# A fused recurrence and MLP kernel on Trainium2: part of the transfers issued by ScalarE, some of them joined, and a new order of all steps

## The chip, the core and the metric

The kernel runs on one core of a Trainium2 chip. The core has a matrix engine (TensorE, "PE", with its weight loads as "PEld"), three engines for elementwise work (VectorE, "DVE"; ScalarE, "ACT"; GpSimd, "POOL") and SyncE ("SP"), which here does nothing but issue transfers. Each engine takes its own instructions in the order in which the program lists them and waits for others through semaphores. Transfers are carried out by 16 DMA engines; an instruction of SP, ACT or POOL issues each of them. The metric is the device time of one execution in microseconds. In the profile L1119 is line 1119 of the kernel.

## What is computed

The inputs are r, k, v, w, a, b with shape (4, 8, 768, 40): batch, heads, time, head size. For each batch and head a 40 x 40 state runs through 768 time steps; the output of all heads, 320 numbers for each of 3072 tokens, goes through an MLP with exact GELU:

```python
for t in range(S):
    y[:, :, t] = np.einsum('bhd,bhde->bhe', rt, state)
    Sa = np.einsum('bhde,bhe->bhd', state, at)
    state_decay = state * wt[:, :, None, :] - np.einsum('bhd,bhe->bhde', Sa, bt)
    state = state_decay + np.einsum('bhd,bhe->bhde', vt, kt)
...
h = x @ w_in                                  # 3072 x 320 by 320 x 2048
g = 0.5 * h * (1.0 + erf(h * inv_sqrt2))
return (g @ w_out).astype(np.float32)         # by 2048 x 320
```

The attention inputs are float32. The MLP's weights arrive as float64 and are taken apart into words and rebuilt as float32 on the core.

## The kernel before

The 768 steps are cut into 12 chunks (c = 0 to 11) of 64. Within a chunk the recurrence is put into matrix form, which needs the inverse of a triangular 64 x 64 matrix for every batch and head. That inverse is made of inverses of 32 x 32 blocks. The work is written as many small *steps*, Python generators that yield wherever another step may be put in between. A token such as `ph3:0` advances step `ph` of chunk 3 by one piece; the number behind the colon names the pair of PSUM banks (0 to 3) that the piece takes. The string ORDER (L30) lists all tokens. The loop at L1231 walks through it, so ORDER sets the order of instructions on every engine. Nothing else schedules.

The steps that matter below, with what they do for chunk c:

- `w`, `a`, `b`, `k`, `v`, `r` (L231 to L277) load inputs; `vp`, `wq`, `bp`, `kp` (L280 to L295) load them again as pairs of time steps, for turned copies that DVE makes in `tv`, `wt`, `tb`, `tk`, `ta`, `tr`. `wi`, `wl`, `wo` load the words of the MLP's weights; `ci` and `co` (to_float, L452) convert them on DVE and ACT.
- `logs`, `sums`, `wt`: logarithms (Ln) of the decays, their running sums, and exponentials (Exp) on ACT. Each change among Ln, Exp and Gelu loads a table on ACT.
- `N`: 32 small products, a masking on DVE (L676), and stores of the 32 x 32 blocks to DRAM (L715). `nb` (L784) loads them back with one block on each partition; `inv` (L788) inverts all of them on POOL in 31 pairs of operations (L799, L801) and stores the result to DRAM (L808, issued by POOL from c = 3 on); `ft` (L822, L826) loads it into Tt. `corner` and `joined` finish the 64 x 64 inverse on PE, DVE and ACT.
- For chunk 0 the inverse is made on PE, DVE and ACT by repeated squaring instead (`sq`, `cornerd`, `joinedd`), since nothing else is there to do yet.
- `A`, `av`, `X`, `sa`, `saT`, `RV`, `M`, `tn`, `yy`, `QY`, `qk`: the products of the recurrence. `state` carries the state to the next chunk.
- `y` (L1041) multiplies the result by the decays on DVE into xt, then shifts parts of it between partitions, so that 320 values fill five groups of 64 partitions: for chunks 1 to 11 with 11 transfers from xt to xt, three at L1071 and eight of 16 KB at L1076. For chunk 0 PE does this.
- `ph` (L1111): the MLP's first product, 64 x 128 tiles in 8 pieces a chunk (L1119), each two followed by GELU on ACT (L1122).
- `po` (L1134): the second product. For chunks 0 and 1 it is plain (L1141); from chunk 2 on seven products of half size and additions on DVE (L1157, L1161 to L1199) take the place of eight. `store` (L1128) writes the output.
- `warm` (L1214): one matrix product whose result nobody reads; `begin`: six of them at the start.

All transfers are issued by SP, except the store of the inverse (POOL from c = 3 on) and six moves of `y11`, which ACT issues. SP takes them in the order of ORDER: one that must wait for its data or for its target to be free holds all that are listed behind it.

Of the kernel before, what the change touches and what calls it, by code (L numbers as in the profile page):

```python
# [10 lines left out]
FP32 = mybir.dt.float32  # L11
# [8 lines left out]
WORDS_BY_ACT = False  # L20
COPIED_BY_ACT = (1, 2)
MOVED_BY_ACT = (11,)
# [11 lines left out]
sq1 sq0 sq1:2 k1 sq0 sq1 warm1:1 N1 sq1 sk0 ci0:0 wi0 sq1:0 N1 ci0 sq1 tr0:1 sq1 ci0 tk0:2 wi0 tk0 sk1 wi0 sq0:3 sq1  # L34
sq0 tr0 A0:2 ci1:1 sq1:0 sq0 ci1 sq1 sq0 nb1 sq1 A0 sq1 wi0 sq0:1 wi0 sq0 RV0:3 sq0 RV0 sq0 wl1 sq1:0 wl1 sq1 inv1 r2
sq0:2 sq1 sq1 sq0 tk1:1 sq0 sq0 sq1:3 tk1 w2 sq1 sq0:0 sq0 cornerd0 placed2 av0:2 ci2:2 placed3 cornerd0:3 ci1 ci2
inv1 nb1 placed1 warm0:1 cornerd0 wl0 ci3:0 wl0 av0 av0:0 r1 ci2 joinedd0:1 av0 joinedd0 tr2:3 placed0 joinedd0 tr2
warm2:2 wi1 a2 ci3 sa0:0 sa0 sa0:1 inv1 sa0 b2 warm5:2 ci4:1 ci9:2 ci4 QY0:3:0 logs2 ci4 k2 qk0 warm7:2 ci9 y0 warm3:1
wi1 state0 wi1 A1:2 wi1 A1 wi1 sums2:1 wi1 inv1 ci9 wo2 sums2:0 sums2 ci3 tv1:3 tv1 tr1:2 sc2 sums2 tn1:0 ci5:1 tn1
ta2:3 ta2 ci5 av1:1 tr1 ci5 sk2 inv1 y0:0 tb2:3 wi1 inv2 ci7:2 tb2 wo6 zeros6 y0:2 ci7 zeros7 y0 y0 tk2:3 av1 ci6:0  # L40
N2:2 ci6 N2 ft1 tk2 co3:1 ph0:0 ft1 ci6 wi1 ph0 corner1:0 N2 ci7 X1:1 corner1:2 corner1 ft1 ph0 X1 ph0:3 wo0 ci8:0
co2:2 ci8 RV1:2 RV1 nb2 warm4:1 ci8 joined1:0 wo9 joined1 wq3 ph0 co0:0 joined1 co0 inv2 ph0 co0 v2 ph0:1 co2 co3
co1:0 sa1:2 co1 sa1 w3 co1 saT1:0 saT1 co3 ph0 co2 wo4 ph0 inv2 ph0:3 co6:0 wt3:1 co6 co7:2 ph0 vp3 co7 ph0 co7
yy1:2:0 logs3 M1:1 M1 tv2:3 wt3 co6 wo8 sums3:1 nb2 sums3 wt3 QY1 zeros5 a3 inv3 tv2 qk1 co4:2 y1 wo15 po0:1 inv2
co5:0 y1 state1 co5 co4 po0 co5 RV2:3 wo10 A2:0 co4 y1 tn2:2 A2 tn2 co9:0 po0 ta3 co9 wt3 inv2 co15:2 bp3 po0 co9 co15
av2:0 co11:1 kp3 co8:0 co11 av2 co11 ph1:2 co8 co8 wo14 inv2 ph1 co10:1 tb3 co10 ph1 wo13 ph1:0 co10 a4 ph1 RV2 ph1
inv4 ft2 co14:0 ph1:2 ta3 co14 wo12 ft2 co14 ft2 N3:3 co15 X2:0 k4 X2 ph1 corner2:1 co13:0 corner2:0 N3 corner2 co13
co12:2 N3 po0 co13 co12 joined2:0 tables0 joined2 k3 joined2 po0 ta4 ph1 co12 sa2:3 nb3 tables0 saT2:0 tk3:1 b3 sa2
sk3 saT2 po0 r3 inv3 yy2:2:3 po0 po0 M2:0 po0 nb3 M2 po0 tv3 ph1:1 inv3 po0 tr3 wq4 ph1 sc3 QY2 w4 qk2 y2 po1:0 state2
bp4 inv3 po1 logs4 b4 A3:2 y2 A3 X3:3 wt4:0 po1 wt4 v3 ph1 wt4 po1 y2 inv3 wt4 po1 po1 ta4 kp4 po1 inv3 vp4 av3:2 tb4  # L50
av3 sums4:1 po1 X3 po1 RV3:2 v4 ws0 sums4 N4:3 N4 inv5 sk4 RV3 ph2:1 N4 sc4 tk4:2 ph2 ft3 ph2 ft3 ph2:3 ws3 nb4 ws1
nb4 ph2 corner3:1 ph2 ft3 ph2:2 inv4 a5 corner3:1 corner3 w5 ph2 ph2 joined3:3 joined3 r4 tn3:1 joined3 tn3 inv4
saT3:3 saT3 sa3:2 sa3 logs5 po1 ph2:1 ta5 bp5 yy3:3:2 M3:0 M3 inv4 tv4 ph2 ph2 tr4 wq5 QY3 qk3 po2:0 po1 sums5:0 sums5
y3 po1 po2:1 state3 y3 po2 inv4 wt5:2 RV4:0 po2:1 po2 wt5 k5 A4:2 po2 A4 tn4:3 y3 tn4 wt5 po2:1 tables1 wt5 po2 po2
inv4 kp5 av4:2 tb5 av4 X4:3 po2 ph3:2 sk5 X4 a6 po2 ta5 ph3 v5 RV4 N5:3 N5 ws2 po2:1 N5 po2 ft4 po2 ph3 ft4 ph3:0 ft4
corner4:0 nb5 tk5:2 ph3 vp5 ph3 corner4:3 ta6 corner4 inv5 nb5 po2 po2:1 po2 joined4:2 joined4 joined4 ph3:0 b5 saT4:3
saT4 sa4:1 r5 inv5 sa4 ph3 ph3 sc5 ph3:2 w6 yy4:3:1 M4:0 M4 tv5 ph3 inv5 ph3 tr5 wq6 QY4 logs6 po3:1 qk4 bp6 state4
po3:0 kp6 y4 po3 po3:2 wt6:0 A5:2 po2 sums6:1 A5 wt6 inv6 k6 inv5 sums6 wt6 y4 po3 wt6 po3 po3:3 po3 po3 tn5:2 y4 tn5
av5:1 tb6 RV5:0 po3 av5 po3 po3:2 ta6 b6 po3 inv5 po3 a7 N6:1 X5:3 N6 X5 N6 sk6 ph4:2 RV5 tk6:1 ph4 ph4 ft5 ta7 ph4:1
ft5 sc6 ft5 A6:3 corner5:0 nb6 r6 inv6 po3 po3:0 po3 corner5:2 A6 corner5 ph4 joined5:0 joined5 ph4 joined5 ph4:2 vp6  # L60
sa5:3 sa5 saT5:0 saT5 inv6 ph4 nb6 ph4 yy5:1:3 w7 M5:0 tr6 tv6 ph4:2 M5 wq7 ph4 inv6 ph4 QY5 v6 logs7 po4:2 qk5 po3 y5
bp7 po4:0 wt7:1 state5 wt7 po4 kp7 po4:0 av6:2 inv7 av6 y5 inv6 wt7 po4 po4 po4:1 wt7 po4 po4 v7 sums7:3 X6:2 y5 po4
ta7 sums7 tb7 po4 po4:0 po4 a8 X6 N7:3 inv6 N7 RV6:1 tk7:2 N7 ph5:2 po4 k7 ph5 ph5 ph5:3 ft6 nb7 ph5 ft6 ph5 nb7
corner6:0 ph5:0 RV6 ft6 inv7 corner6:2 po4 corner6 tn6:3 r7 tn6 po4:1 po4 joined6:2 ta8 joined6 joined6 ph5 inv7 vp7
ph5 sa6:3 sa6 saT6:1 saT6 ph5:2 po4 yy6:0:3 bp8 M6:1 M6 inv7 tr7 ph5 ph5 tv7 QY6 po5:1 wq8 qk6 y6 po5:1 state6 y6 po5
po5:2 inv7 po5 wt8:0 A7:2 y6 RV7:0 A7 wt8 tn7:3 RV7 tn7 wt8 vp8 inv7 po5 po5:1 po5 wt8 po5 X7:2 av7:0 inv8 av7 tb8 sk7
kp8 po5 ta8 b7 inv9 po5 po5:3 po5 a9 po5 N8:0 N8 ft7 ph6:1 N8 ph6 ph6 ft7 ta9 ph6:3 ft7 corner7:1 X7 ph6 tk8:2 nb8 ph6
corner7:0 nb8 corner7 sc7 ph6:1 r8 inv8 joined7:2 joined7 joined7 po5 po5:3 po5 sa7:0 sa7 saT7:2 saT7 bp9 ph6 inv8 po5
ph6 ph6:3 w8 yy7:0:2 M7:1 M7 tv8 ph6 ph6 wq9 inv8 QY7 logs8 po6:0 qk7 tr8 v8 state7 po6:1 y7 v9 po6 wt9:1 tn8:3 y7 tn8
A8:0 inv8 A8 wt9 X8:2 sums8:3 po6:2 po6 sums8 wt9 y7 po6 po6:0 po6 wt9 po6 av8:1 av8 kp9 RV8:3 po6 tb9 b8 inv8 po6  # L70
# [10 lines left out]
corner10 po9:2 vp11 po9:2 joined10:3 joined10 joined10 po9 nb11 sa10:0 inv11 sa10 r11 saT10:1 po9:1 saT10 tn10:3 tn10
po9 po9 po9:0 yy10:1:3 v11 M10:2 M10 tv11 po9 inv11 po9 po9 logs11 QY10 qk10 y10 po9 po9:2 y10 state10 po9 po9 X11:0
y10 sums11:1 sums11 A11:3 A11 inv11 po9 po9:2 po9 tn11:1 tr11 tn11 av11:3 po9 av11 RV11:2 X11 b11 inv11 RV11 ph10:1
k11 ph10 ph10 sc11 ph10:3 sk11 ft11 ph10 ft11 ph10 ft11 ph10:0 corner11:0 ph10 ph10 corner11:2 corner11 ph10:1
joined11:3 joined11 joined11 ph10 ph10 saT11:0 saT11 po10:2 po10:2 yy11:3:1 M11:0 M11 po10 po10:1 po10 QY11 po10 qk11
y11 po10:0 y11 po10 po10 y11 po10 y11 po10 po10:2 y11 y11 y11 po10 y11 po10 po10 po10:1 po10 po10 ph11:3 ph11 ph11
ph11:0 ph11 ph11 ph11:2 ph11 ph11 ph11:1 ph11 ph11 po11:0 po11:3 po11 po11:2 po11 po11 po11:0 po11 po11 po11 po11
po11:2 po11 po11 po11 po11:1 po11 po11
"""


@with_exitstack
def kernel(
    ctx: ExitStack,
    tc: tile.TileContext,
    r: bass.AP,
# [100 lines left out]

    raws = {}  # L200
# [1067 lines left out]
```

## Time and profile before

| | |
|---|---|
| runs of the kernel before | 668.63, 669.81 and 672.28 us |
| their median | 669.81 us |
| profiled execution, first to last instruction (span) | 661.8 us |
| median above that span | 8.0 us |
| granted TensorE clock over the span | 0.999 |
| transfers issued by SP, ACT and POOL | 774, 6 and 18 |
| bytes moved | 79.41 MB, mean 120 GB/s |

The profile of one execution tells only its span; the 8.0 us are what lies around it, by the runs. The page gives each engine's busy time; issuing a transfer is not counted as busy, but the timeline has it as rows of SPq and ACTq. Waits are listed by who waited for whom, with the total, the number and the longest. A row of the timeline has the start, the time to its last end, engine, line, operation, output and inputs, shape, and how many instructions it joins. One float32 product stands there as two instructions. Its end is modelled and reaches into the next product, so the distance from one row's start to the next row's is the better price.

### The profile page before, as it was taken

The page shows a single profiled execution, that of the slowest core. Times are in us where ns is not written, and L with a number is a line of the kernel's source. Part 1 is how long each engine was busy: PE and PEld are TensorE (multiplying, and loading weights), DVE is VectorE, ACT ScalarE, POOL GpSimd, SP SyncE. Part 2 cuts the span into 40 slices and gives each one's busy share as a digit, 9 for nine tenths or more (in the row PEclk, how much of TensorE's full clock was granted, in tenths as well). Part 3 has the DMA queues.
Part 4 walks back from the last instruction along what each step waited for, and adds up shares of the span by engine and source line. Part 5 has one row for each costly group of instructions (what it writes and reads, how often), then busy time and mean ns, then how long its engine had stood idle before and what let it go on. Part 6 is the DMA issues. An engine that isn't in the chain of part 4 may idle for free.

```text
span 661.8 us, 30753 instructions
## 1 busy us (share of the span) xinstructions
PE 646.7 (98%) x13768; PEld 567.3 (86%) x13768; DVE 416.0 (63%) x536; ACT 239.3 (36%) x305; POOL 367.7 (56%) x799
## 2 busy tenths in 40 slices
PE   8889999999999999999999999999999999999997
PEld 4777788777778988998998998998988999998987
DVE  1778989976483874983863963863765674632313
ACT  4355646432424622522522422515253242232020
POOL 6158536706857837846838836847823874840000
PEclk9999999999999999999999999999999999999999
DMA  9989675696676476764775485675685465450100
GB/s 136 164 192 176 158 167 132 153 159 146 116 132 134 105 137 134 140 116 112 145 141 107 94 153 124 119 147 110 115 146 111 103 121 102 86 101 3 42 1 21
DMA packets 300708, 79.41 MB, mean 120 GB/s; under 512 B 288584, under 2 KB 293328, under 8 KB 300576
## 3 DMA queue, kind: packets, MB, share of 16 engines
q1 hardware_dynamic: 299512, 74.92, 58.3%
q0 software_dynamic: 864, 2.36, 1.8%
q8 instruction: 108, 1.77, 1.1%
q14 instruction: 24, 0.20, 0.1%
q10 hardware_dynamic: 200, 0.16, 0.1%
HBM read 64.09 MB, written 9.70 MB: 112 GB/s over the span
## 4 chain that ended last, share of the span: by engine, by line
PE 82%; DVE 8%; SPq 5%; issue 2%; DMA 1%; ACT 0%; DVEq 0%; ACTq 0%
PE duo L1119 29%; PE duo L149 25%; PE duo L1157 22%; PE duo L1141 4%; PE duo L557 2%; SPq L213 2%; SPq L227 1%; DVE conv L466 1%; SPq L1076 1%; DVE conv L472 1%; DMA spare<-in_a_dram 1%; DVE conv L458 1%; DVE conv L457 1%; DVE aT L588 1%; DMA rows<-in_b_dram 0%
## 5 line engine op out<-in xcount | busy, mean ns | idle before, releaser
L1119 PE MATMUL duo<-xt,w_in_sb 64*128 64x256 f32 x1920 | 218.8, 381 | 1.4 <-issue 1.4
L1119 PEld LDWEIGHTS duo<-xt,w_in_sb 64*128 64x128 f32 x1920 | 182.5, 187 | 23.9 <-issue 2.3
L799 POOL TENSOR_TENSOR tmp<-W,Nb 128x56 f32<-128x56 f32 (+22 forms) x155 | 71.8, 464 | 79.9 <-DMA Nb<-N 51.4
L1122 ACT ACTIVATE gt<-duo 128x1024 f32<-128x1024 f32 x48 | 49.2, 1025 | 143.0 <-PE duo L1119 132.1
L799 POOL TENSOR_TENSOR tmp<-rT,Nb 128x56 f32<-128x56 f32 (+22 forms) x155 | 70.2, 453 | 52.8 <-DMA Nb<-N 41.0
L1157 PE MATMUL duo<-w_out_sb,gt 128*128 128x160 f32 x640 | 93.3, 303 | 0.0
L1157 PEld LDWEIGHTS duo<-w_out_sb,gt 128*128 128x128 f32 x640 | 87.6, 190 | 2.4 <-issue 0.8
L801 POOL TENSOR_TENSOR W<-W,tmp 128x56 f32<-128x56 f32 (+22 forms) x155 | 71.8, 463 | 12.1
L801 POOL TENSOR_TENSOR rT<-rT,tmp 128x56 f32<-128x56 f32 (+22 forms) x155 | 68.4, 441 | 12.1
L1157 PE MATMUL duo<-extra,conv 128*128 128x160 f32 x320 | 46.0, 301 | 0.0
L1157 PEld LDWEIGHTS duo<-extra,conv 128*128 128x128 f32 x320 | 43.8, 190 | 1.4 <-issue 0.5
L1141 PE MATMUL duo<-w_out_sb,gt 128*128 128x320 f32 x128 | 36.9, 440 | 0.1
L1161 DVE TENSOR_TENSOR os<-os,duo 128x160 f32<-128x160 f32 x40 | 12.7, 318 | 31.9 <-PE duo L1157 28.0
L1141 PEld LDWEIGHTS duo<-w_out_sb,gt 128*128 128x128 f32 x128 | 23.6, 190 | 10.1 <-issue 0.5
L1164 DVE TENSOR_TENSOR conv<-gt 128x1024 f32<-128x1024 f32 x10 | 12.7, 1266 | 27.5 <-ACT gt L1122 27.5
L605 POOL TENSOR_TENSOR rows<-rows,w_tile 128x640 f32<-128x640 f32 x9 | 15.8, 1761 | 25.0 <-DMA Nb<-N 16.0
L676 DVE TENSOR_TENSOR SM<-duo,left_upper 128x1024 f32<-128x1024 f32 x11 | 13.4, 1221 | 24.4 <-PE duo L149 24.4
L931 DVE COPY Tt<-duo 32x512 f32<-32x512 f32 x11 | 7.6, 689 | 30.4 <-ACT Tt L931 30.3
L149 PE MATMUL duo<-rT,late 40*64 40x64 f32 x1472 | 26.1, 219 | 0.0
L149 PEld LDWEIGHTS duo<-rT,late 40*64 40x64 f32 x1472 | 23.7, 135 | 2.1 <-issue 2.1
L1122 ACT ACT_TABLE_LOAD x14 | 18.0, 1283 | 19.1 <-DVE os L1161 14.7
L1157 PE MATMUL duo<-extra,gt 128*128 128x160 f32 x160 | 23.9, 302 | 0.0
(222 smaller groups left out, 1092.0 us busy)
## 6 DMA issues: line engine op xcount, KB each, us to landing
Nb<-N SPq DMA_DIRECT2D x40, 128.0 KB
VR<-in_v_dram SPq DMA_DIRECT2D x24, 160.0 KB
out_dram<-os SPq DMA_DIRECT2D x48, 80.0 KB
rows<-in_b_dram SPq DMA_DIRECT2D x22, 160.0 KB
rows<-in_k_dram SPq DMA_DIRECT2D x22, 160.0 KB
w_out_sb<-in_moe_w_out_dram SPq DMA_DIRECT2D x5, 640.0 KB
w_tile<-in_w_dram SPq DMA_DIRECT2D x36, 80.0 KB
Tt<-inv SPq DMA_DIRECT2D x44, 64.0 KB
```

Source lines behind the costliest of these rows:

```text
L149: nc.tensor.matmul(o, lhsT, rhs, start=first, stop=True, skip_group_check=True)
L213: nc.sync.dma_start(out=t[half(e)].rearrange("p g h d -> p (g h) d")[:, :, :D], in_=rows_of(src, c, e))
L557: nc.tensor.transpose(pt[:, g, n], src(g, n), ident)
L605: (nc.gpsimd if c in SCALED_BY_POOL or c >= NB else nc.vector).tensor_tensor(to, raws.pop((c, "k")), t["rw"], ALU.mult)
L676: nc.vector.tensor_tensor(to, pt, upper.unsqueeze(1).to_broadcast([P, NBL, C]), ALU.mult)
L799: eng.tensor_tensor(t, W[:, :nr, j:j + 1].to_broadcast([P, nr, rest]), Nb[:, j:j + 1, j + 1:].to_broadcast([P, nr, rest]), ALU.mult)
L801: eng.tensor_tensor(W[:, :nr, j + 1:], W[:, :nr, j + 1:], t, ALU.add)
L1119: nc.tensor.matmul(pt[:, x, s], w_in_sb[half(x), kt, p * P:(p + 1) * P], xt[half(x), kt], start=kt == 0, stop=kt == NK - 1)
L1122: nc.scalar.activation(gt[:, 4 * q:4 * q + 4].rearrange("p (x s) t -> p x s t", x=2), pt, ACT.Gelu)
L1141: nc.tensor.matmul(pt[:, g], gt[:, f, g * P:(g + 1) * P], w_out_sb[:, f], start=f == 0, stop=f == NF - 1)
L1157: nc.tensor.matmul(pt[:, n, :DM // 2], l_[:, f], r_[:, f], start=f == 0, stop=f == NF // 2 - 1)
L1161: nc.vector.tensor_tensor(to, one_, other, ALU.add)
```

## The change

Four things change in the code; the rest is the order.

A mark `*` in front of a token makes every transfer of that piece be issued by ACT instead of SP. The constants that did this for single cases go.

Loads yield more often: `r`, `vp` and the other loads of pairs, `a`, `w`, and N's stores are listed in two to four pieces, each with two transfers. The transfers themselves stay the same.

Some transfers are joined. From chunk 3 on `nb` loads each half of the partitions with one transfer instead of two. In chunks 1 to 10 the fifth group of xt (eight transfers of 16 KB before) is written to DRAM with two transfers and read back with two.

ORDER is new throughout. Both orders hold the same pieces of work for the engines.

```diff
-WORDS_BY_ACT = False
-MOVED_BY_ACT = (11,)
...
+    raws, queue = {}, [nc.sync]
...
+    def load(out, in_):
+        queue[0].dma_start(out=out, in_=in_)
...
 def nb(c):
...
         for z in range(2):
-            for par in range(2):
-                nc.sync.dma_start(out=Nb[par * n:(par + 1) * n, rows_of_blocks[z]], in_=blk[:, rows_of_blocks[z]])
+            for par in (range(2) if c < NT else (z,)):
+                rows_ = rows_of_blocks[z] if c < NT else slice(0, BL)
+                load(Nb[par * n:(par + 1) * n, rows_], blk[:, rows_])
             yield
...
 def y(c):
...
         for x in range(2):
             own, other = x * HP, (1 - x) * HP
-            eng = nc.scalar if x and c in MOVED_BY_ACT else nc.sync
             for to, n in ((0, NP - 1), (NP - 1, 1)) if x else ((0, NP),):
                 at = (to + x) % NP
-                eng.dma_start(out=xt[own + D:own + HP, to:to + n], in_=xt[other:other + REST, at:at + n])
...
-            for i in range(NP):
-                n = D - REST
-                eng.dma_start(out=xt[own + i:own + HP:NP, NP], in_=xt[other + REST:other + D, i])
...
+                load(xt[own + D:own + HP, to:to + n], xt[other:other + REST, at:at + n])
+            yield
+        if c == NCH - 1:
+            for i in range(NP):
+                for x in range(2):
+                    own, other = x * HP, (1 - x) * HP
+                    load(xt[own + i:own + HP:NP, NP], xt[other + REST:other + D, i])
+                yield
+            return
+        last = dram.tile([2, D - REST, NP, TB], FP32, tag="last", name="last")
+        for x in range(2):
+            load(last[x], xt[x * HP + REST:x * HP + D, :NP])
+        yield
+        for x in range(2):
+            load(xt[half(x), NP], last[1 - x].rearrange("p i t -> (p i) t"))
+        yield
...
     for token in ORDER.split():
-        name, *at = token.split(":")
+        queue[0] = nc.scalar if token[0] == "*" else nc.sync
+        name, *at = token.strip("*").split(":")
```

The order before and after, its first lines and its last:

```diff
-w0 begin6 pads1 consts0 w1 tails1 b1 inv1 zeros1 begin6:0 logs0 zeros2 wi0 gaps0 b0 consts0 logs1 tails0 pads0 a0
-consts0 sums0:1 gaps1 sums0:2 zeros0 v0 sums0 zeros4 warm6:3 pads3 pads2 sums1:0 zeros3 shifts0 sums0 sc0 a1 sums1:3
-sums1 tb0:2 sums1 sc1 wi0 ta0:1 r0 tb0 ta0 tb1:3 N0:0 N0 tb1 wi0 ta1:2 k0 ta1 N0 tv0:1 sq1 v1 tv0 sq0 N1:3 sq0 sq0:0
...
-ph11:0 ph11 ph11 ph11:2 ph11 ph11 ph11:1 ph11 ph11 po11:0 po11:3 po11 po11:2 po11 po11 po11:0 po11 po11 po11 po11
-po11:2 po11 po11 po11 po11:1 po11 po11
+begin6 tails0 gaps1 w0 *w1 *b0 begin6:0 logs0 logs1 a0 inv1 consts0 warm5:0 sums0:0 b1 r0 r0 zeros1 sums0:1 sums0
+gaps0 a1 pads0 wi1 shifts0 k0 pads1 sums1:2 sums1:3 ta0:1 sums0 sc0 sums1 sums1 ta0 tb0:0 warm1:3 r1 sc1 tb0 zeros2
+N0:1 tb1:0 tails1 *v0 N0 consts0 tr0:2 tb1 ta1:3 wi1 sq0 sq1 sq0 sq0:0 N0 ta1 pads3 k1 sq0 sq1 sq1:1 pads2 N1:3 wi0
...
+ph11 ph11 ph11:1 ph11 ph11 po11:0 po11:2 po11 po11:2 po11 po11 po11:1 po11 po11 po11 po11 po11:2 po11 po11 *po11
+po11:1 warm2:2 po11 po11 warm4:1
```

More of the change, by code (lines that the diff above doesn't have):

```diff
@@ L36 @@
[L36 to L50, printed above, removed]
@@ L66 @@
[L66 to L70, printed above, removed]
@@ L81 @@
[L81 to L85, printed above, removed]
@@ new lines @@
+sums11 y10 inv11 po9:3 sk11 po9 po9 tn11:0 tr11 tn11 *po9 sc11 po9:2 po9 ph10:0 ph10 ph10 ph10:2 ph10 ph10 ph10:0 ph10
+tv11 ph10 ft11 ph10:2 ph10 corner11:2 corner11:0 RV11:3 corner11 ft11 ft11 X11 RV11 *po9 ph10 joined11:0 joined11
+joined11 po10:2 po10:1 po10 po10:0 po10 po10 saT11:0 saT11 yy11:1:2 M11:3 po10:0 M11 QY11 qk11 po10 po10 y11 *y11 y11
+*y11 *y11 y11 po10 po10 po10:2 *y11 y11 po10 po10 *po10 po10:1 po10 *po10 ph11:2 ph11 ph11 ph11:1 ph11 ph11 ph11:2
+ph11 ph11 ph11:1 ph11 ph11 po11:0 po11:2 po11 po11:2 po11 po11 po11:1 po11 po11 po11 po11 po11:2 po11 po11 *po11
@@ L209, in by_64 @@
         return plain(t)[:, :G * H * HP].rearrange("p (n d) -> p n d", d=HP)
+    def load(out, in_):
+        queue[0].dma_start(out=out, in_=in_)
     def fetch(c, n, src, t):
         for e in range(2):
-            nc.sync.dma_start(out=t[half(e)].rearrange("p g h d -> p (g h) d")[:, :, :D], in_=rows_of(src, c, e))
+            load(t[half(e)].rearrange("p g h d -> p (g h) d")[:, :, :D], rows_of(src, c, e))
         raws[c, n] = t
     def fetch_pairs(n, src, c, t, placed):
+        raws[c, n] = t
         rows_ = slice(c * C // 2, (c + 1) * C // 2)
@@ L223, in fetch_pairs @@
                         pairs = src[G * e + x].rearrange("h (s y) d -> s h (y d)", y=2)
-                        nc.sync.dma_start(out=to[:, e::2], in_=pairs[rows_, :, cols])
+                        load(to[:, e::2], pairs[rows_, :, cols])
+                    yield
                 else:
                     pairs = src.rearrange("b (i x) (s y) d -> x s (b i) (y d)", x=2, y=2)[x]
-                    nc.sync.dma_start(out=to, in_=pairs[rows_, :, cols])
-        raws[c, n] = t
+                    load(to, pairs[rows_, :, cols])
+            if not placed:
+                yield
     @step
@@ L238, in w_ @@
                 for g in range(G):
-                    nc.sync.dma_start(out=to[half(e ^ g), g],
-                                      in_=w[G * e + g, :, c * C:(c + 1) * C].rearrange("h t d -> t h d"))
-        raws[c, "w"] = t
-        yield
+                    load(to[half(e ^ g), g], w[G * e + g, :, c * C:(c + 1) * C].rearrange("h t d -> t h d"))
+                raws[c, "w"] = t
+                yield
     @step
@@ L247, in a_ @@
             fetch(c, "a", a, by_64(spare if c == 1 else paired["a"]).rearrange("p (g h) d -> p g h d", g=G))
-            raws[c, "a"] = by_64(spare if c == 1 else paired["a"]).rearrange("p (g h) d -> p g h d", g=G)
+            yield
         else:
-            fetch_pairs("a", a, c, paired["a"], False)
-        yield
+            yield from fetch_pairs("a", a, c, paired["a"], False)
     @step
@@ L265, in v_ @@
         for e in range(2):
-            nc.sync.dma_start(out=VRs[c % 2][half(e)].rearrange("p g q m d -> p (g q m) d")[:, :, :D], in_=rows_of(v, c, e))
+            load(VRs[c % 2][half(e)].rearrange("p g q m d -> p (g q m) d")[:, :, :D], rows_of(v, c, e))
         yield
@@ L271, in r_ @@
         if c >= NT:
-            fetch_pairs("r", r, c, paired["r"], True)
+            yield from fetch_pairs("r", r, c, paired["r"], True)
         else:
@@ L423, in wi @@
                     if m:
-                        (nc.scalar if x and WORDS_BY_ACT else nc.sync).dma_start(out=words[to:to + m, i], in_=words_from(first, [(4 * wd, m)], x, c))
+                        load(words[to:to + m, i], words_from(first, [(4 * wd, m)], x, c))
                 yield
@@ L431, in wl @@
         for x in range(2):
-            (nc.scalar if x and WORDS_BY_ACT else nc.sync).dma_start(out=words[half(x)], in_=words_from((1 - x) * D + REST, [(4 * wd, D - REST), (2 * D * 4 * wd, NP)], x, c))
+            load(words[half(x)], words_from((1 - x) * D + REST, [(4 * wd, D - REST), (2 * D * 4 * wd, NP)], x, c))
             yield
@@ L447, in wo @@
         at = (c // 2 % 2 * (NF // 2) + 2 * (c // 4) + c % 2) * P
-        nc.sync.dma_start(out=second_words(c, n).rearrange("p (f m) -> p f m", f=n),
-                          in_=src[at:at + n * P].rearrange("(f p) m -> p f m", p=P))
+        load(second_words(c, n).rearrange("p (f m) -> p f m", f=n), src[at:at + n * P].rearrange("(f p) m -> p f m", p=P))
         yield
@@ L714, in N @@
                 at = j * HP + z * BL
-                nc.sync.dma_start(out=blk[j, z].rearrange("n s t -> s n t"),
-                                  in_=flat(N)[at:at + BL, :, z * BL:(z + 1) * BL])
-        blocks[c] = blk
-        yield
+                load(blk[j, z].rearrange("n s t -> s n t"), flat(N)[at:at + BL, :, z * BL:(z + 1) * BL])
+            blocks[c] = blk
+            yield
     def parts_of_N(c):
@@ L807, in inv @@
         for par in range(2):
-            (nc.gpsimd if c >= INVERSES_BY_POOL else nc.sync).dma_start(out=to[par], in_=W[par * n:(par + 1) * n])
+            (nc.gpsimd if c >= INVERSES_BY_POOL else queue[0]).dma_start(out=to[par], in_=W[par * n:(par + 1) * n])
         stored[c] = iv
@@ L821, in ft @@
                 at = j * HP + z * BL
[L822 to L823 removed]
+                load(flat(Tt_tile)[at:at + BL, :, z * BL:(z + 1) * BL], iv[j, z].rearrange("n s t -> s n t"))
             yield
         for j in range(2):
[L826 to L827 removed]
+            load(odd_corners()[lo[j]], iv[j, 1].rearrange("(n z) s t -> z s n t", z=2)[1])
         yield
@@ L1130, in store @@
             row = (G * e + g) * S + c * C
-            nc.sync.dma_start(out=out[row:row + C], in_=oss[g][half(e)].rearrange("p z d -> p (z d)"))
+            load(out[row:row + C], oss[g][half(e)].rearrange("p z d -> p (z d)"))
     @step
```

116 lines of the change are left out of this document (66 added, 50 removed).

## The prediction

> **What bounds the kernel now.** I read the page's shares first, then PE's waits, then busy time by stretch, and last single rows of the timeline.
>
> ```profile
> span 661.8 us, 30753 instructions
> ...
> PE 646.7 (98%) x13768; PEld 567.3 (86%) x13768; DVE 416.0 (63%) x536; ACT 239.3 (36%) x305; POOL 367.7 (56%) x799
> ```
>
> PE is the bound: 15.1 us of the span are not PE's, 10.9 us as gaps before its last product ends at 657.6 and 4.2 us behind it (last add, last store).
>
> ```profile
> PE duo L149 <- issue: 2.7, 4, 1.1
> PE duo L149 <- DVE w_in_sb L1220: 1.5, 1, 1.5
> PE duo L1119 <- issue: 1.4, 1, 1.4
> PE duo L149 <- ACT w_in_sb L871: 1.4, 2, 1.0
> PE duo L149 <- DVE aT L588: 1.2, 3, 0.6
> PE duo L557 <- ACT wpT L525: 0.9, 1, 0.9
> PE duo L557 <- DMA spare<-in_a_dram: 0.4, 1, 0.4
> ```
>
> Only the last line waits for a transfer. About 4.1 us are "issue", which no semaphore ended; 8 of the 10.9 us lie before 70 us.
>
> ```profile
> core 0: us, PE busy (x) PEld busy (x) DVE busy (x) ACT busy (x) POOL busy (x), PEclk, DMA share, GB/s
> 10.00:20.00 10.00, 8.45 (x162) 6.32 (x162) 2.88 (x3) 5.44 (x6) 2.68 (x12) 1.00 1.08 149
> 20.00:30.00 10.00, 8.94 (x209) 7.42 (x205) 8.38 (x14) 4.51 (x6) 1.54 (x1) 1.00 1.08 151
> 60.00:70.00 10.00, 8.95 (x257) 6.77 (x251) 9.93 (x16) 4.94 (x6) 8.67 (x18) 1.00 0.94 220
> 100.00:150.00 50.00, 48.24 (x977) 39.40 (x974) 45.55 (x84) 22.55 (x31) 23.97 (x56) 1.00 0.70 149
> 400.00:450.00 50.00, 50.00 (x1055) 45.79 (x1056) 30.84 (x36) 16.15 (x20) 34.29 (x70) 1.00 0.67 131
> ```
>
> The columns to compare are PE and DVE. At 400 PE is full and every other engine has room: nothing can be won there by earlier transfers. Up to 150 us DVE is nearly full too, and up to 30 us the DMA engines are (share 1.08). SP, which the page does not count, issues 774 transfers in 514.5 us of its own time, 26 to 27 of each 30 us in the steady part; it is tight, but PE does not wait for it.
>
> ```profile
> 11.10 1.02 PE L149 MATMUL duo<-cum_m,ident 128*128 128x512 f32 x2
> ...
> 324.94 4.61 PE L1157 MATMUL duo<-extra,conv 128*128 128x160 f32 x32
> ...
> 553.77 2.44 PE L1157 MATMUL duo<-w_out_sb,gt 128*128 128x160 f32 x16
> 556.14 0.75 PE L149 MATMUL duo<-Tt,Js 32*32 32x32 f32 x64
> ...
> 578.30 2.86 SPq L1076 DMA_DIRECT2D xt<-xt  x4
> ...
> 619.03 3.20 ACTq L1076 DMA_DIRECT2D xt<-xt  x4
> ```
>
> Read these as prices. A product alone takes 2.37 us to the next row (553.77 to 556.14); two together 4.54 (324.94 to 329.48): each separate run costs 2 x 2.37 - 4.54 = 0.20 us. One warm step is 1.02 us. The four small moves were issued in 2.50 to 2.86 us by SP (0.63 each over all 84), 3.20 us by ACT (0.80 each).
>
> **The change part by part.** The span of this execution, 661.8, stands 8.0 below the median of the runs, 669.81; I sum on the span and add 8.0. A step's "position" is the sum of the PE rows listed before it, waits left out.
>
> PE's work. Both orders list the same PE steps. Listed neighbours of one tile shape form runs. po (po2 to po11) and the two early output blocks are cut into 48 runs before and 40 after: 8 x 0.20 = -1.6 us. ph goes from 41 runs to 44: +0.6. Transposes and the 40-row products lose a run each, 0.06 by 1.043 against 0.982 us: -0.1. Sum **-1.1**.
>
> Warm steps. Before, all eight stand at positions 10 to 83. After, five stand early, warm0 at 299, warm2 and warm4 behind the last product. Their cover is the 4.2 us tail: warm2 1.02, then the 0.32 us add that frees warm4's PSUM pair, then 1.02, is 2.4. The path loses 2 x 1.02. If early slots turn into waits it loses 0; the row at 11.10 has work right behind it, with no gap, so I take **-2.0**. Without the tail's cover they cost +2.0.
>
> The first 25 us. Three waits (wpT L525 0.94, aT L588 0.61, a_dram 0.42) are 1.97 us together. After, ta0 stands ahead of tb0, and a1 is issued behind six loads on SP, with w1 and b0 on ACT and v0 later. What is late next is ACT: two Exp for c=0, two for c=1, a table load and the copy of tb0 are 1.28 + 2 x 0.70 + 2 x 1.03 + 1.01 = 5.75 us, against 1.16 + 1.34 + 1.05 + 1.05 + 1.02 = 5.6 us of listed PE work: about 0.6 us of wait with the hops. **-1.4**, between 0 and -2.0.
>
> [...]
>
> Later waits on DVE (aT 0.23 and 0.38, Tt 0.60) have slightly longer covers after: I take **-0.3**, between +1 and -1.
>
> Transfers. Steps that are split issue the same transfers. y1 to y10 issue 7 instead of 11 (40 fewer), nb3 to nb11 two instead of four (18 fewer): 798 become 740, 18 on POOL as before. 213 go to ACT, 509 stay on SP: 509 x 0.665 = 338 us instead of 514.5. ACT takes 213 x 0.665 (SP's mean) to 0.91 (the mean of ACT's own six): 142 to 194 us; by its nearest row, 0.80, 170. Counting Ln, Exp and Gelu along the lists, ACT's table loads fall from 44 to 39: -6.4 us. ACT is then occupied about 239 - 6 + 170 = 403 of 660 us. All this is costed at **0**: PE's own queue covers it, and gelu, ACT's main work, waited 132 us for PE. If the cover goes, each chunk of 64 steps has some 18 ACT issues, 14 us.
>
> The corner of xt through DRAM adds a trip: its write must land before the read is issued. Nearest row: N's stores end 2.9 us before the load behind them starts (341.6, 344.5). Multiplication 1.3, shifts 2.4, write 1.3 + 2.9, read 1.3 + 2.9 are 12 us in a line, some of it side by side. From y to ph of one chunk lie 12.8 to 25.1 us of PE before, 9.5 (c = 10) to 21.9 after; the last shape is used 1.7 us into ph. c = 10 is about even. y11 keeps its 11 moves, 7 of them on ACT: 1.5 for the multiplication, 7 x 0.80 + 0.3 for a copy between them, 2.9 to land are 10.3 us, against 8.8 from qk11's end to ph11 (11.0 before) and the 1.7. Both 0, at worst +1 each.
>
> POOL's inverse. From N's stores to the first ft lie on average 50.4 us of PE before (44.8 to 55.0), after 54.3 (48.5 to 61.1). The trip took 45 to 52 us (c = 9: 439.7 to 484.6). c = 7, with 48.5, can be short by 3.5, but corner7 stands 14 us behind ft7: 0.
>
> Sum: -1.1 - 2.0 - 1.4 - 0.3 = -4.8. The span becomes 657.0, the time **665.0**; from 661.5 (all gaps but the first 1.5 and the "issue" go: -8.3) to 666.4.
>
> **The rivals.**
>
> DVE binds the start. Up to the words that ph0's second half needs, DVE has 65.6 us of work listed before position 86.7, after 62.8 before 78.0: nearly one for one from 25 us on. From 24 us (5 us of it done) the other 58 take 64 us at the density of 100 to 150 us (45.55 of 50), 71 at 82%, that of 20 to 60 us. They end at 88 or 95, where the forecast has PE arrive at about 85: +3 or +10, times 668 or 675. For it: 9.93 at 60 to 70. Against it: loads that arrive in another order may pack DVE more tightly.
>
> ACT stands behind a waiting transfer, the case on the slow side. Its place: N's stores (one of two by ACT, c = 1 to 11), behind DVE's mask, with gelu next on ACT. Before, SP stood 30.5 us behind one add, so an issuer does stand still. If the mask waits behind a 2.4 us pair on DVE, and half reaches PE, 11 x 1.2 = 13 us: 678. Slower than before from 4.8 / 11 = 0.44 us a chunk on, clearly from 0.74. Against it: those ACT stretches have mostly 2 to 10 us of listed PE work before the next ACT step. [...]
>
> The change does less than it says. SP's relief is worth nothing where PE is full, and waits take what warm steps and runs gave up: 669, no change.
>
> **How the numbers follow.** 0.5% (3.3 us) is about what a measurement of this kernel tells from no change. As forecast 0.44; better than 661.5, 0.08; DVE at the higher density or nothing gained (666.5 to 673) 0.25; DVE at the lower density 0.08; ACT standing 0.15. So faster 0.52, same 0.25, slower 0.23. The range leaves 0.05 below 660.5 and 0.13 above 677: it holds both DVE cases and the first half of ACT's.
>
> **What would show it.** Right: fewer L1157 runs, 39 table loads, two warm rows behind the last product, gaps of PE near 9 us, most before 100 us, SP issues near 340 us. Wrong: PE waits for ACT's gelu after an ACT-issued row (ACT standing), PE waits for w_in_sb L473 or Tt at 60 to 115 us (DVE), or PE waits at L1119 for xt (the corner's trip).

## The result and the profile after

The changed kernel is slower: 699.29 us median (697.02 to 705.94), against 669.43 us for the kernel before (668.63 to 672.28); the ratio is 1.0465, 95% interval 1.0405 to 1.0525. The forecast was 665.0 with 677.0 as its upper end.

The profiled execution of the changed kernel has a span of 704.2 us and took 705.94 us, so it is the slowest of the four; the profile of before shows one that lies below its kernel's median. Of the 42.4 us between the two profiles some 12 are thus spread between executions. First the page's shares (the first line, and engine by engine busy time, share and instructions).

```profile
span 704.2 us, 30682 instructions
...
PE 663.9 (94%) x13768; PEld 581.2 (83%) x13768; DVE 410.5 (58%) x536; ACT 232.4 (33%) x300; POOL 358.7 (51%) x799
```

The 42.4 us between the two spans are all PE's. Its gaps before the last product grow from 10.9 to 37.7 us (+26.7), its busy time from 646.7 to 663.9 (+17.2), and the tail behind it shrinks by 1.5. The busy time is mostly the same work at a lower clock: the granted clock was 0.5 for 37.6 us of the changed kernel's span, of which half, 18.8 us, is about what was added; in before it was 0.5 not once until the last product had ended. The gaps grow late: from 4.1 to 3.5 us up to 30 us, from 4.0 to 6.8 from there to 100 us, and from 2.8 to 27.3 us behind that. What PE waited for (total, times, longest):

```profile
PE duo L152 <- issue: 9.8, 8, 3.4
PE duo L152 <- DVE conv L909: 6.0, 3, 3.4
PE duo L1126 <- DMA xt<-last: 5.9, 5, 2.3
PE duo L152 <- ACT w_tile L502: 3.9, 1, 3.9
PE duo L152 <- DVE aT L591: 3.5, 3, 2.4
PE duo L152 <- DVE SM L679: 1.8, 1, 1.8
```

The second line is `corner` waiting until `ft` has brought the inverse; the third is `ph` waiting for xt's corner. Neither stood in the list of before. Both are transfers that came late, and SP's queue says why. First three lines of what SP waited for in before (the two longest, and the longest wait for a transfer), then the changed kernel:

```profile
SPq L1131 <- DVE os L1161: 39.8, 6, 30.5
SPq L1071 <- DVE xt L1045: 21.3, 1, 21.3
...
SPq L822 <- DMA inv<-rT: 1.5, 1, 1.5
```

```profile
SPq L215 <- DVE xt L1046: 37.9, 4, 33.4
SPq L215 <- DVE os L1168: 36.2, 2, 34.1
SPq L215 <- DVE late L564: 33.3, 8, 7.9
SPq L215 <- DVE st L1098: 21.0, 4, 16.4
SPq L215 <- DMA out_dram<-os: 18.4, 4, 7.4
SPq L215 <- DMA r_pairs<-in_r_dram: 17.2, 9, 3.7
SPq L215 <- DMA a_pairs<-in_a_dram: 15.9, 6, 7.3
SPq L215 <- DMA N<-N: 15.2, 6, 4.3
SPq L215 <- DMA N<-spare: 12.5, 6, 5.5
```

In before SP waited for results of DVE and POOL and for almost nothing else; its waits for transfers are 4.5 us in 6. Here they are 169.3 us in 87, and many of these transfers are none of its business: a load of inputs waits for a store of output. SP now issues for 325.1 us in place of 514.5, and PE waits for transfers all the same.

The timeline has the mechanism in one place. These are the rows of SP's queue and of ACT from 292 to 303 us (start, duration, engine, line, what):

```profile
296.13 0.81 SPq L215 DMA_DIRECT2D v_pairs<-in_v_dram  x2
297.05 4.16 SPq L215 DMA_DIRECT2D a_pairs<-in_a_dram  x2
301.31 1.70 SPq L215 DMA_DIRECT2D N<-N  x1
```

```profile
292.92 0.88 ACTq L215 DMA_DIRECT2D a_pairs<-in_a_dram  x2
...
298.42 0.86 ACTq L215 DMA_DIRECT2D N<-N  x2
```

By the pairs beside them (0.81 and 0.88 us) SP's two loads into a_pairs should take some 0.8 us; the row is 4.16 us long, because the second was issued at 300.90. The trace gives each transfer the semaphore that counts its landing. SP and ACT share eight of them (100, 102, 104 to 109). Number 104 was used by ACT's a_pairs at 292.92, by ACT's store of N at 298.78, and then by SP's a_pairs, whose recorded wait is on 104 and ended at 300.89, when the store had landed. ACT's stores of N could start at 298.42 only, since DVE's mask ended at 298.40. So a load of inputs by SP stood 3.5 us behind a store by ACT that stood behind DVE, and all of SP's transfers behind it stood too. Among these is chunk 5's `ft`: the inverse had landed at 293.12, SP issued the two transfers that `corner` needs from 305.06 on, they landed at 311.75 and 312.67, and PE's `corner` waited 2.37 us, until 313.5. Over the whole trace SP lost 75.5 us in 33 such waits for a semaphore that ACT's transfer still held, in before none. This counts the waits that the transfer's own instruction carries; with those that stand in an instruction just ahead of it they are about 138 us in 56.

### The profile page after: what moved, and what is told of

It reads as the page before. It is cut to its first block, busy times and chain, and to the rows that moved or that the text cites. A ratio compares the mean times of both kernels' runs of the same rounds, so it can differ in the third digit from the quotient of the medians.

```text
span 704.2 us, 30682 instructions
## 1 busy us (share of the span) xinstructions
PE 663.9 (94%) x13768; PEld 581.2 (83%) x13768; DVE 410.5 (58%) x536; ACT 232.4 (33%) x300; POOL 358.7 (51%) x799
## 5 line engine op out<-in xcount | busy, mean ns | idle before, releaser
L1126 PE MATMUL duo<-xt,w_in_sb 64*128 64x256 f32 x1920 | 226.7, 387 | 6.2 <-DMA xt<-last 5.9
L1126 PEld LDWEIGHTS duo<-xt,w_in_sb 64*128 64x128 f32 x1920 | 185.9, 190 | 32.8 <-DMA xt<-last 8.2
L802 POOL TENSOR_TENSOR tmp<-rT,Nb 128x56 f32<-128x56 f32 (+22 forms) x155 | 64.7, 417 | 94.4 <-DMA Nb<-N 82.7
L1164 PEld LDWEIGHTS duo<-w_out_sb,gt 128*128 128x128 f32 x640 | 89.1, 193 | 3.5 <-issue 1.3
L804 POOL TENSOR_TENSOR W<-W,tmp 128x56 f32<-128x56 f32 (+22 forms) x155 | 68.6, 442 | 12.1
L1148 PE MATMUL duo<-w_out_sb,gt 128*128 128x320 f32 x128 | 36.9, 440 | 0.0
L1148 PEld LDWEIGHTS duo<-w_out_sb,gt 128*128 128x128 f32 x128 | 23.6, 190 | 10.0 <-issue 1.0
L608 POOL TENSOR_TENSOR rows<-rows,w_tile 128x640 f32<-128x640 f32 x9 | 14.2, 1581 | 33.6 <-ACT w_tile L525 21.9
L152 PE MATMUL duo<-rT,late 40*64 40x64 f32 x1472 | 28.3, 224 | 1.5 <-issue 1.4
L152 PEld LDWEIGHTS duo<-rT,late 40*64 40x64 f32 x1472 | 25.4, 138 | 4.1 <-issue 3.3
L909 DVE STREAM_TRANSPOSE conv<-Tt 128x512 f32<-128x512 f32 x11 | 7.8, 706 | 32.8 <-DMA Tt<-inv 32.8
L1164 PE MATMUL duo<-extra,gt 128*128 128x160 f32 x160 | 26.2, 320 | 0.5 <-issue 0.5
L1171 DVE TENSOR_TENSOR conv<-gt 128x1024 f32<-128x1024 f32 x10 | 12.8, 1276 | 23.5 <-ACT gt L1129 23.5
```

The source lines that it names most:

```text
L152: nc.tensor.matmul(o, lhsT, rhs, start=first, stop=True, skip_group_check=True)
L608: (nc.gpsimd if c in SCALED_BY_POOL or c >= NB else nc.vector).tensor_tensor(to, raws.pop((c, "k")), t["rw"], ALU.mult)
L802: eng.tensor_tensor(t, W[:, :nr, j:j + 1].to_broadcast([P, nr, rest]), Nb[:, j:j + 1, j + 1:].to_broadcast([P, nr, rest]), ALU.mult)
L804: eng.tensor_tensor(W[:, :nr, j + 1:], W[:, :nr, j + 1:], t, ALU.add)
L909: nc.vector.transpose(L, flat(Tt_tile)[:, :, :BL])
L1126: nc.tensor.matmul(pt[:, x, s], w_in_sb[half(x), kt, p * P:(p + 1) * P], xt[half(x), kt], start=kt == 0, stop=kt == NK - 1)
```

## The experiments

All ratios are to runs of the kernel before on the same chip, with 95% intervals. Line numbers shift by a few between the kernels.

### Which part costs

**All by SP, order and joins kept.**

```diff
-        queue[0] = nc.scalar if token[0] == "*" else nc.sync
+        queue[0] = nc.sync
```

> The changed kernel with its order and its joined transfers, but every transfer issued by SP (the marks are ignored). Theory A, two issuers hold each other up: SP's and ACT's transfers share eight completion semaphores that are taken in turn in the order of the program, so a transfer waits until the eighth before it has landed, whichever engine issues that one; ACT's late ones then hold SP. It expects most of the 29.5 us to be gone: 670 to 680 us, PE gaps of 11 to 17 us. Theory B, the new order lists transfers too late for whoever issues them: 692 to 705, and rather worse, since SP has 480 us to issue in place of 325. Theory C, the corner of xt through DRAM: unchanged, 695 to 702.

677.17 us, ratio 1.011 (1.0072 to 1.0148). SP's waits for the other queue are gone; its waits for DVE are 145.1 us (178.5 in the changed kernel, 100.6 in before). The marks thus cost some 22 of the 30 us.

**The order alone**, by SP, with nb's four loads and the eight small moves of xt back in place.

```diff
+                load(Nb[par * n:(par + 1) * n, rows_of_blocks[z]], blk[:, rows_of_blocks[z]])
...
+            for i in range(NP):
+                load(xt[own + i:own + HP:NP, NP], xt[other + REST:other + D, i])
+            yield
```

> The new order alone: every transfer by SP, no joined transfers, the same 780 transfers as the kernel before. Theory A: 668 to 682. Theory B: 692 to 710. Theory C: 670 to 700, it says nothing of the order, but the loss that it names is gone.

681.76 us, 1.0195 (1.0146 to 1.0244): the order costs 13 us by itself, and the joins win about 4.6 of them back (this interval and the one before it just touch). SP issues 534.8 us here, more than 27 of each 30 us in most of the steady part.

**Order and marks without the joins** (the same lines undone, the marks kept).

> The changed kernel with its order and its marks, but the joined transfers undone: nb by four transfers, the fifth group of xt by eight moves instead of the trip through DRAM. Theory C (the trip makes PE wait for xt, 5.9 us of waits and a stretch at half clock): 685 to 692. Theories A and B: 697 to 706, since 58 more transfers are issued and nothing that they name is undone.

711.68 us, 1.0605 (1.0541 to 1.0669). All three theories missed: undoing the joins costs 9 to 12 us here. PE waits 10.0 us for xt in this run, where no trip is left, and 5.9 with the trip: the trip is not what makes xt late.

**The marks alone, in the order of before.** Each piece that is marked in the new order is marked here.

```diff
-inv2 ph1 co10:1 tb3 co10 ph1 wo13 ph1:0 co10 a4 ph1 RV2 ph1 inv4 ft2 co14:0
+inv2 ph1 co10:1 tb3 co10 ph1 wo13 ph1:0 co10 a4 a4 ph1 RV2 ph1 inv4 *ft2 co14:0
```

> The kernel before, with its own order and no joined transfers, but ACT issues the transfers of the same pieces of work that are marked in the new order (114 pieces). Theory A: the two issuers hold each other up here as well, 685 to 705, with SP waiting for transfers of other work. Theory B: about as before, 667 to 673. Theory C: about as before.

683.28 us, 1.0224 (1.0167 to 1.0281): 15 us, with 44.7 us of SP's waits for ACT's semaphores. So the harm of the marks does not need the new order.

### How ACT's transfers hold SP

**A quarter of the transfers by ACT, picked by their number.** I wanted two semaphores to be ACT's alone in the first run and all eight mixed in the second.

```diff
+        (nc.scalar if n % 8 // 2 == 3 else nc.sync).dma_start(out=out, in_=in_)
...
+        (nc.scalar if n % 8 // 2 == n // 8 % 4 else nc.sync).dma_start(out=out, in_=in_)
```

> The changed kernel with its order and its joined transfers, but in place of the marks every transfer whose number n in the program has n % 8 in (6, 7) is issued by ACT, 180 of 722. Two of the eight completion semaphores are then ACT's alone and six SP's alone, so a transfer never waits on a semaphore for one of the other queue. Theory A1, the shared semaphores couple the two queues: 670 to 682, about as with SP alone (677), with hardly any wait of SP for a transfer. Theory A2, ACT is simply a bad issuer (it stands between its own work and its transfers, and what it issues comes late): 688 to 705.

> As the run before, the same share and the same pairs (one pair of every four, 180 transfers), but the pair moves on by two places every eight transfers, so that each of ACT's transfers waits on its semaphore for one of SP's, and two of every eight of SP's for one of ACT's. Theory A1: 690 to 705, ten or more above the run before. Theory A2: the same as the run before, within 4 us.

683.04 us, 1.020 (1.0114 to 1.0286), and 694.85 us, 1.0361 (1.0286 to 1.0437). The edit did not do what it was for: in both traces ACT's transfers use all eight semaphores. With SP as the only issuer each semaphore comes back with every eighth transfer of the list (714 times of 714 in the run all by SP); with two issuers it comes back after 1 to 18, so the semaphores are not dealt in the listed order. SP's waits for ACT are 75.9 and 72.0 us, as in the changed kernel, and yet the first run stands only 6 us above the one all by SP. The total of these waits is thus no price: what one costs depends on what stands behind it. The pair tells only that it matters *which* transfers ACT gets; separate semaphores stay untried.

**Transfers that nobody needs.** This isolates the wait. Behind each of the 48 GELUs of the kernel before stands one transfer of 160 bytes, by ACT in the first run, by SP in the second.

```diff
             nc.scalar.activation(gt[:, 4 * q:4 * q + 4].rearrange("p (x s) t -> p x s t", x=2), pt, ACT.Gelu)
+            tiny = dram.tile([1, D], FP32, tag="tiny", name="tiny")
+            nc.scalar.dma_start(out=tiny, in_=r[0, 0, :1])
```

> The kernel before, its order and all its transfers as they are, and 48 more transfers of 160 bytes to a place that nobody reads, each issued by ACT right behind one of the 48 GELUs. No useful transfer is on ACT. Theory A1 (a transfer waits on its completion semaphore for the transfer that had it before, whichever queue issued that one): the tiny ones come as late as the GELUs, SP stands behind them, 676 to 695, with more than 30 us of SP's waits for the other queue. Theory A2 (ACT is a bad issuer of what others need): 668 to 673, as 48 x 0.6 = 29 us more on ACT are hidden.

> The same 48 tiny transfers, at the same places in the program, issued by SP. This is what 48 more transfers cost when one queue issues all: 29 us more for SP, which is busy 514 of 662 us already. Theories A1 and A2: 668 to 676; under A1 below the run before, under A2 at or above it.

By ACT 702.81 us, 1.0487 (1.0414 to 1.056); by SP 685.84 us, 1.0258 (1.0192 to 1.0324). ACT has none of the useful transfers but the six of y11 that it had before, and 48 times 160 bytes are nothing beside 79.41 MB; yet this costs as much as the whole change. From SP's and PE's waits of the first run:

```profile
SPq L715 <- DMA tiny<-in_r_dram: 10.2, 5, 3.5
SPq L227 <- DMA tiny<-in_r_dram: 10.0, 4, 4.6
...
SPq L822 <- DMA tiny<-in_r_dram: 5.7, 4, 2.4
SPq L1133 <- DMA tiny<-in_r_dram: 4.5, 2, 3.0
```

```profile
PE duo L149 <- DVE conv L908: 12.3, 6, 4.0
PE duo L149 <- DMA Tt<-inv: 4.8, 5, 1.8
...
PE duo L149 <- ACT late L981: 1.4, 1, 1.4
PE duo L149 <- ACT w_in_sb L871: 1.2, 2, 0.9
```

SP, storing N (L715) or loading inputs (L227), waits for a tiny transfer that it has no use for: 36.9 us in 19 waits by the semaphores. PE then waits 17.1 us for the inverse, and for ACT hardly longer than in before (2.6 against 2.3 us). So it is not ACT's own work that suffers. The second run has its own lesson: 48 more issues on SP, whose issues take 564.2 us in place of 514.5, cost 17 to 18 us. SP is nearly as critical as PE.

**Which marks.** First only those on pieces that wait for results (48 stay), then only those on loads of inputs (66 stay). A stretch of the order shows both edits.

```diff
-av3 vp4 y2 vp4 X3:1 ta4 sc3 N4:0 N4 y2 *po0 RV3:3 RV3 *N4 N4 inv3 y2 po0 po1 po1 *vp4 po1 po1
+av3 vp4 y2 vp4 X3:1 ta4 sc3 N4:0 N4 y2 *po0 RV3:3 RV3 *N4 N4 inv3 y2 po0 po1 po1 vp4 po1 po1
...
-av3 vp4 y2 vp4 X3:1 ta4 sc3 N4:0 N4 y2 *po0 RV3:3 RV3 *N4 N4 inv3 y2 po0 po1 po1 *vp4 po1 po1
+av3 vp4 y2 vp4 X3:1 ta4 sc3 N4:0 N4 y2 po0 RV3:3 RV3 N4 N4 inv3 y2 po0 po1 po1 *vp4 po1 po1
```

> The changed kernel with the marks kept only on pieces that wait for results (N, nb, ft, inv, y, po: 48 of 114); the inputs are all SP's. If SP loses time to ACT's late transfers through the shared semaphores, these are the marks that do it: 688 to 700. If any mark costs alike: 677 + 48/114 x 22 = 686. If ACT's inputs are what comes late: 675 to 681.

> The changed kernel with the marks kept only on loads of inputs (66 of 114), all results moved by SP. First case as above: 675 to 685. Any mark alike: 690. ACT's inputs late: 692 to 700.

706.43 us, 1.0574 (1.0515 to 1.0634), and 686.94 us, 1.0268 (1.0199 to 1.0336). The 48 late marks cost 29 us over all-SP's 677, more than all 114 together; the 66 on inputs 10. With the late ones, SP's queue shows

```profile
SPq L214 <- DMA N<-N: 36.9, 6, 10.8
...
SPq L214 <- DMA N<-spare: 28.1, 5, 10.0
SPq L214 <- DMA xt<-xt: 22.9, 9, 6.1
SPq L214 <- DMA out_dram<-os: 17.8, 6, 7.7
```

and PE waits 15.2 us for `xt<-last`, which SP then issues late. N, xt and out are just the results that ACT was told to move.

### The joins, and what a lighter SP is worth

**Both joins in the order of before**, by SP; the same with a quarter of the transfers on ACT; and nb's join alone.

```diff
-            for par in range(2):
-                nc.sync.dma_start(out=Nb[par * n:(par + 1) * n, rows_of_blocks[z]], in_=blk[:, rows_of_blocks[z]])
+            for par in (range(2) if c < NT else (z,)):
+                rows_ = rows_of_blocks[z] if c < NT else slice(0, BL)
+                nc.sync.dma_start(out=Nb[par * n:(par + 1) * n, rows_], in_=blk[:, rows_])
```

> The kernel before with the joined transfers alone, all by SP (the read of the corner listed five pieces behind its write); six of y11's moves, ACT's before, are SP's here too. If the joins are a gain in any order (681.8 to 677.2 in the new one): 660 to 667. If they only help where SP is late: 667 to 671. If the trip through DRAM costs PE waits: 672 to 680.

> The order of the kernel before with the joined transfers (the read of the corner listed five pieces behind its write), and ACT issuing n % 8 in (6, 7). Theory A1: 660 to 672. Theory A2: 680 to 690, as with the marks in this order (683).

> The kernel before with nb's loads joined from chunk 3 on, and nothing else: 18 transfers fewer, 13 us less for SP to issue. If SP's tightness costs this kernel anything: 664 to 668. If not, 668 to 671. If the larger transfer lands later and POOL's inverse with it: 672 to 676.

682.34 us, 1.0197 (1.0118 to 1.0276); 683.93 us, 1.021 (1.0131 to 1.029); 682.39 us, 1.0221 (1.0153 to 1.0289). Eighteen transfers *fewer* cost 15 us. The reason is where the pieces stand. In the order of before, steps of the inverse stand between nb's two pieces in chunks 3, 5, 6, 9, 10 and 11. The old first piece brings half the rows of both halves of the partitions, all that those steps read; the joined first piece brings all rows of one half. In these three runs those steps therefore take the other half's rows from the chunk before (their numbers are then not the recurrence's; the runs serve as timings), and the second load must wait until POOL has read them (SP's queue, nb's join alone):

```profile
SPq L823 <- DMA inv<-rT: 15.5, 4, 5.8
SPq L785 <- POOL rT L802: 12.4, 4, 5.4
SPq L785 <- POOL tmp L800: 12.2, 2, 6.6
```

SP stands 24.6 us behind POOL at nb (L785), and everything listed behind it is late. In the new order no such step stands between the two pieces.

**The trip alone in the order of before; then the trip and nb's two joined loads side by side.** The piece that reads stands five pieces behind the one that writes. The second run adds the last lines.

```diff
+            load(last[x], xt[x * HP + REST:x * HP + D, :NP])
+        yield
...
+            load(xt[half(x), NP], last[1 - x].rearrange("p i t -> (p i) t"))
...
+            for par in (range(2) if c < NT else (0, 1) if z == 0 else ()):
```

> The kernel before with the trip of xt's corner through DRAM alone (40 transfers fewer, 25 us less for SP; the read five pieces behind its write; ACT keeps half of y11). If SP in step with PE is what bounds this order too (48 tiny transfers more cost 18 us): 660 to 666. If before has no use for a lighter SP: 667 to 672. If SP standing for the write's landing (20 us in ten waits where this was tried with nb joined) costs more than it saves: 673 to 682.

> As the run before, and nb's loads joined with both halves at the place of the first piece (58 transfers fewer in all). If the late second half was what made joined nb slow (682): within 4 us of the run before, or below it. If the joined transfer itself is slow: 5 us or more above it.

Both kernels leave all of y11 to SP; the expectations are wrong there. 662.77 us, 0.9918 (0.9884 to 0.9952), and 663.51 us, 0.9936 (0.9902 to 0.997): the trip is the only part of the change that wins against the kernel before. 40 issues fewer give 5.5 us; nb's join, with both halves in the place of the first piece, costs nothing and adds nothing. The page of the first:

```profile
span 660.1 us, 30684 instructions
...
PE 648.2 (98%) x13768; PEld 567.9 (86%) x13768; DVE 415.0 (63%) x536; ACT 239.1 (36%) x305; POOL 367.0 (56%) x799
```

PE's gaps are 7.7 us and no wait for xt is among its listed waits. The trip through DRAM is hidden here.

### The clock, and the warm steps

**Two warm steps ahead of each of eight waiting places of the changed kernel.**

```diff
-A5:3 ph3:1 A5 a6 corner4:2 ph3 corner4
+A5:3 ph3:1 A5 a6 warm20:2 warm21:2 corner4:2 ph3 corner4
...
-X11:1 *y10 av11 sums11:0
+X11:1 *y10 av11 warm34:0 warm35:0 sums11:0
```

> The changed kernel with two more warm steps (2.0 us of PE's work) ahead of each of eight places where PE waited 1.8 to 3.9 us in its profile: corner4, corner5, N7, ph6, ph7, N11, X10, sums11. The gaps there were 19.3 us and can hold about 15 of the 16.3 us of warm steps. If the halved clock behind such gaps costs what the profile shows (30.7 us at 0.5 behind four of them, so 15 us): 683 to 691 and one or two stretches at half clock left. If the clock is no part of the loss: 697 to 703.

703.25 us, 1.0508 (1.0452 to 1.0564): no gain. The clock itself answered as expected. Two stretches of the changed kernel, then the same two of this one (PE busy first, the granted clock before the last two columns):

```profile
240.00:260.00 20.00, 16.57 (x406) 14.02 (x406) 9.39 (x12) 3.38 (x4) 7.15 (x18) 0.86 0.66 108
...
340.00:365.00 25.00, 22.62 (x311) 21.72 (x311) 17.30 (x20) 5.93 (x7) 10.21 (x19) 0.80 0.64 123
```

```profile
240.00:260.00 20.00, 19.82 (x497) 16.07 (x497) 11.25 (x16) 5.80 (x9) 7.86 (x16) 1.00 0.77 125
...
340.00:365.00 25.00, 23.39 (x406) 20.21 (x407) 14.73 (x18) 5.94 (x8) 7.86 (x19) 1.00 0.76 125
```

The time at half clock behind 250 us fell from 30.7 to 6.8 us, by my estimate worth half the difference, 12 us; the gaps fell by 12.8 us. But 16.3 us of filler were added, and half-clock time before 120 us rose by 10.2 us. In the profiles 3.2 us are left as gain, in the timed runs nothing. So the clock follows PE's gaps and adds to the loss in the profile, but warm steps in the gaps win no time: what PE waits for stays as late as it was.

**Two warm steps moved behind the last product**, in the kernel before, and on top of the trip.

```diff
-co2:2 ci8 RV1:2 RV1 nb2 warm4:1 ci8
+co2:2 ci8 RV1:2 RV1 nb2 ci8
...
-po11:1 po11 po11
+po11:1 warm2:2 po11 po11 warm4:1
```

> The kernel before with warm2 and warm4 moved from positions 25 to 70 us to behind the last products, as in the new order, and nothing else. By the prediction's term: 2.0 us less, 665 to 668 (ratio 0.997). If the two steps stood in waits or kept the clock up: 668 to 674.

> The order of before with the trip of xt's corner, all by SP (y11 too, as in j1_trip_in_before, which left no transfer on ACT although its expectation says that ACT keeps half of y11), and warm2 and warm4 moved as in the run before. If the terms add up: 659 to 662 (ratio 0.989). If the order is so closely fitted that an early shift of 2 us costs elsewhere: 663 to 672.

669.51 us, 0.998 (0.9944 to 1.0016), and 664.71 us, 0.993 (0.99 to 0.996). Neither 2.0 us nor 0 is excluded by the first; on top of the trip nothing was gained.

## Why the prediction was wrong

**The failed step** is "Transfers ... All this is costed at 0: PE's own queue covers it". Two things were wrong with it. SP had no cover: 48 tiny issues more cost 17 to 18 us, 40 fewer gave 5.5. Set against the places in the order, SP issued its transfers of before 0.5 to 2.1 us *behind* PE (medians of 50 us stretches, from 100 to 600 us), and 0.7 to 5.2 with the 48 more. (This distance is no price either: with 40 fewer it is 0.3 to 2.9, and in the changed kernel, which lists the transfers at other places, SP is mostly ahead of PE.) "Tight, but PE does not wait for it" read the absence of waits as slack; it was a fit. And the queues were taken as independent. They share eight completion semaphores, so SP inherits ACT's lateness: 75.5 us of waits. The term, put at 0, measured some 22 us for the marks; the other 8 to 9 us are the order's and the joins', and their step is not found.

**The rival "ACT stands behind a waiting transfer"** named the right place, N's stores, and the wrong victim. It priced GELU being held at 678, a loss from 0.44 us a chunk on. ACT stood 29.1 us ahead of N's stores (9 waits), and PE's waits for ACT came to 6.0 us in all (2.3 in before), 3.9 of them one wait for the logarithms of the decays at 615 us. Ahead of these ACT had issued four loads of r, from 609.40 to 613.20, the last of them for 2.4 us without a wait that the trace records; with everything by SP this wait of PE is 0.4 us. There, once, ACT's transfers held up ACT's own work. As far as the waits show, the rest of the harm went through SP: N's stores are among the marks that cost 29 us by themselves. Its chance of 0.15 and its price were both too low. What the prediction lacked is that an issuer's wait may be for another queue's transfer: SP's row of 4.16 us ended when ACT's store of N had landed.

**The base.** "8.0 around it" was wrong: the changed kernel's profiled execution took 1.7 us more than its span, and executions of before 1.8 to 1.9. The profile of before shows an execution of some 663.6 us (661.8 and 1.8), so most of the 8.0 was spread between executions. That moves the basis, not the sign.

**PE's work, -1.1**: about right. PE's busy time in the changed kernel, less half of its 37.6 us at half clock, is an estimated 645.1 against 646.7. ACT's instructions fell by the five table loads.

**Warm steps, -2.0**: the two rows are there behind the last product, and the tail is 1.5 us shorter; as a gain in time it was not shown. **The first 25 us, -1.4**: PE's gaps before 30 us fell by 0.6. **Later waits on DVE, -0.3**: they grew. aT went from 1.2 to 3.5 us, Tt from 0.6 to 1.5, and 1.8 for SM is new, +5; with SP alone these three still make 6.0 us of the 17.5 us of gaps, against 1.8 in before. That is the rival "DVE binds the start" in part, but its longest wait (2.4 us) lies at 331 us. Why the order costs its 9 to 13 us without ACT was not taken apart further.

**ACT's 170 us of issues**: 125.4 us, 0.58 each, not 0.80. **The corner, 0**: right by itself, a gain even; its 5.9 us of PE waits come from late issue. **POOL's inverse, 0**: of the 6.0 us at `corner` 2.4 are chunk 5's late `ft` (above), not POOL. But 3.4 are chunk 4, where the inverse itself was late: SP's stores of N came 6 us after ACT's (193.1 against 186.9), POOL took 44.5 us from the last load of `nb` to its store (35.0 in before), and that store landed at 249.59, when SP had stood 6.4 us for it.

## What to carry to other kernels

An issuing queue that causes no waits may still have no slack; a few dozen tiny transfers more can show it (48 cost 17 to 18 us here). Price a transfer moved to another engine by who will wait for that engine's place in its own work. Here two queues drew on one set of eight completion semaphores and were coupled by it: SP lost 75.5 us in 33 waits for a semaphore that one of ACT's transfers still held, often for work of no concern to the one waiting, and late results were the worst thing to hand to a second issuer (29 us for 48 marks, against 10 for the 66 on inputs). Before joining transfers, look at which steps are listed between the pieces: a join that saves issues can also turn a partial load into a wait (24.6 us of SP's time at `nb` here).

## What the runs showed of the hardware that I had not expected

PE's granted clock fell to 0.5 in stretches of 3.41 us or a multiple of it: in the profile of the changed kernel, up to its last product, four of 6.83 us and one of 10.24, in other runs also 3.41. Of the five in the changed kernel four began within a gap of PE (1.83 to 3.94 us long) and one 0.02 us behind a gap of 3.40; in the other runs the latest began some 2.6 us behind one. In the kernels run here a gap of 0.97 us was enough once (at 46.5 us of the first run with a quarter of the transfers on ACT, with no other gap in the 10 us before it), while one of 2.37 us at 311 us of the changed kernel had no effect: the length of a gap alone did not tell.

The spread between executions of one kernel goes with this clock: of 65 executions of the kernel before, the 18 at a granted clock of 1.000 have a median of 666.6 us, the 16 at 0.995 or less one of 671.2. Which of the two comes first, the runs do not show.
